# A backward pass on one TensorE: late loads and stores put on Sync's queue, parameter steps spread from another group on, and the opening of the last pass reordered

## The chip, the cores and the metric

The kernel runs on one core of one Trainium2 chip. The metric is the device time of one execution in microseconds. Engines are named as in the profile: PE (TensorE, with PEld for its weight loads), DVE (VectorE), ACT (ScalarE), POOL (GpSimd) and SP (Sync, which here only issues DMAs).

## The reference, cut to what matters

The reference is one block of a network and its gradients, with L = 2048 positions, D = 576 channels, N = 128 states, F = 4608 hidden units:

```
xn  = layernorm(x)
s   = ssm(xn)                      # convolution with K = sum_n C exp(dt A l) dt B, plus xn * Dskip
h   = silu(xn @ w1) * (xn @ w3)    # gate G, up U
out = x + s * silu(h @ w2)
outputs: out, and the gradients of x, A, B, C (re, im), log_dt, Dskip, w1, w3, w2
```

Three parts of the gradient matter here. With go the gradient at the output of h @ w2: gh = go @ w2.T; GG and GU, the gradients at xn @ w1 and xn @ w3, come from gh, G and U elementwise; grad w2 = h.T @ go, grad w1 = xn.T @ GG, grad w3 = xn.T @ GU. The gradient at xn is GG @ w1.T + GU @ w3.T (plus the convolution's part), followed by the layernorm's backward. And the gradients of A, B, C and log_dt need, for every channel, a sum over positions of the kernel's gradient times powers exp(dt A l).

## The kernel before, in words

A forward part (to some 700 us) writes G and U, the two hidden products, to DRAM by groups of 256 hidden units, position-major within the group. What follows is `backward` (L1521), in two stages.

**The group loop (L1599).** F is worked in NG = 18 groups of 256 units (numbered 0 to 17 here). For group gi:

- `phase6_group` (L1743) makes gh in four parts h0 to h3 (L1765, 40 matmuls each two parts), multiplies it into the prepared tiles gu and gg (L1783), and stores them as GU and GG (L1788, four DMAs on SP). After that comes the stage "stored".
- `phase6_grad2` (L1793), called at h1 and h3 for the group's two blocks of 128 units, makes grad w2 (L1806), copies it out of PSUM on ACT (L1810) and stores it to out_12 (L1811).
- `phase6_grad13` (L1813) makes grad w3 (out_11) and grad w1 (out_10), 64 matmuls each (L1826), with copies on ACT (L1828) and one store each (L1832), and a tail for the last 64 channels (L1836, L1838) whose two small stores (L1844, L1845) are issued at the beginning of the next group.
- Meanwhile the next group is prepared (`phase6_prep`, L1724): ACT computes silu(G) and its derivative (L1733, L1736), DVE the products with U (L1729, L1730).

For that, each group loads 1 MB of G (`phase6_load_gg`, L1704, for the next group, issued at the head of a group) and 1 MB of U (`phase6_load_h`, L1688, for the group after the next, issued after h3). In the kernel before, these two loads and all gradient stores are issued by POOL, chained in the order of the program (`gp`, L142). SP issues the rest: the rows of w2 (L1665), their transposes w2T (L1686, `nat_transpose`), the GU and GG stores, and from group GP = 11 on the loads for the parameter steps and the weight transposes wA ("end" of groups 11 to 15). From group 11 on `self.chain` holds SP's issues too in the order of the program (`sp`, L139); an engine's issue waits in that order for what it needs.

**Parameter steps.** `param_step` (L1230) does half a chunk of 8 channels: 8 matmuls (L1400), then on DVE two products (L1405) and two sums (L1408). There are 72 steps. A chunk's data are a DMA transpose qT, two loads gz and a load pz (`param_loads`, L1379), issued two chunks ahead. Steps stand at h1, h3, out_11, out_10 and "end" of the groups from 11 on, and in groups 12 to 15 at "stored" as well; in group 17 at h1, h3, out_11 and twice in the extra work at "stored". 39 steps are done in the groups, 33 in the last pass. The final blocks (`phase5_step`) turn finished sums into outputs.

**The last pass (`phase6_inputs`, L1852).** For each of 16 tiles of 128 positions it sums 72 pieces (36 of GG with w1.T, 36 of GU with w3.T; two matmuls of 288 columns each, L1876) in PSUM and then does the layernorm's backward. The activations of a tile (`acts`, one DMA transpose for GG and one for GU, `load_acts`, L1678) go into one of two buffers, so tile i+2's GG half can be loaded only when tile i has read its GG half. The weights come as transposed pieces (`load_piece`, L1668), which take over buffers of the group loop as these come free. The order of `steps` (L1857) is that in which the pieces were loaded, `sides` (L1858) is first all GG, then all GU. Tiles 0 and 1 take the order `steps`, all others `sides`. As L1888 to L1903 have it, tiles 0 and 1 are interleaved: each 49 pieces (what was loaded by the group loop), then each 9, then tile 0's last 14 and tile 1's last 14, with the loads for tiles 2 and 3 and the held parameter loads (`param_flush`, L1247) between. `stops` (L1910) says after which pieces a tile has parameter steps: three for tiles 3, 4, 6 and 8, four for tile 2, two for the others.

Of the kernel before, what the change touches and what calls it, by code (L numbers as in the profile page):

```python
# [17 lines left out]
P = 128  # L18
# [82 lines left out]
class K:  # L101
# [1128 lines left out]
    def param_step(self):  # L1230
# [3 lines left out]
        if self.half == 0:  # L1234
            for ch in range(2):
                self.loaded[ch] = self.param_loads(ch)
# [10 lines left out]
    def param_flush(self):  # L1247
        hold, self.hold = self.hold, None
        for ch in hold:
            self.loaded[ch] = self.param_loads(ch)  # L1250
# [270 lines left out]
    def backward(self, T0, TG, TQ, TC, TX, gctx, mats):  # L1521
# [11 lines left out]
        FA, GP = 14, 11  # L1533
        with ExitStack() as out:
# [22 lines left out]
            self.tail = None  # L1557
            self.at(T0 - TG)
# [40 lines left out]
            for gi in range(NG):  # L1599
                self.chain = gi >= GP  # L1600
# [103 lines left out]
    def phase6_load_gg(self, gi, inp):  # L1704
        gg = inp.tile([P, self.cfg.LT, self.FG], BF16, name="gg_n")
        self.gp(lambda: self.nc.gpsimd.dma_start(out=gg[:], in_=self.G_dram[gi]))
# [86 lines left out]
    def phase6_grad2(self, gi, fl, hn, gwp, ps_gw):  # L1793
# [6 lines left out]
        if True:  # L1800
# [10 lines left out]
            self.gp(lambda: nc.gpsimd.dma_start(out=aps["out_12"][fi * P:(fi + 1) * P, :], in_=gw2[:]))  # L1811

    def phase6_grad13(self, gi, gg_n, gu_n, gwp, ps_gw):  # L1813
# [7 lines left out]
        for (nat, oname) in ((gu_n, "out_11"), (gg_n, "out_10")):  # L1821
            gw = gwp.tile([P, nfull, FG], BF16, name="gw13", tag="gw13")
            for c in range(nfull):
# [6 lines left out]
                if (oname, c) in (("out_11", 2), ("out_10", 1)):  # L1830
                    yield oname
            self.gp(lambda: nc.gpsimd.dma_start(out=aps[oname][0:nfull * P, fb:fb + FG].rearrange("(c p) f -> p c f", p=P),  # L1832
                                                in_=gw[:]))
# [9 lines left out]
        def tail():  # L1843
            self.gp(lambda: nc.gpsimd.dma_start(out=aps["out_10"][nfull * P:D, fb:fb + FG], in_=gw[0:rem, :]))  # L1844
# [7 lines left out]
    def phase6_inputs(self, T2, TX, wT, acts, pool):  # L1852
# [7 lines left out]
        with pool(name="l_sb", bufs=2) as sb, pool(name="l_s1", bufs=1) as s1, \  # L1860
# [34 lines left out]
            for i in range(2):  # L1895
                product(i, opened[i][0], n1, n2, ())
# [160 lines left out]
```

## Time and profile before

| | |
|---|---|
| median of three timed runs | 1762.47 us (1759.99 to 1764.70) |
| the profiled execution | 1769.46 us |
| its span, first to last instruction | 1767.7 us |
| groups 11 to 17 of the group loop | 1161.2 to 1441.6 us of the span |
| the last pass, to its last matmul | 1441.6 to 1760.2 us |

Times in the profile are microseconds from the span's beginning. A row of a timeline has start, duration, engine, line, operation, output<-inputs and count, and in brackets how long the engine was idle before it and what ended the idle time. Rows of engine SP (SPq) are DMA issues; they last as long as SP is held by them. "To landing" is the time from a DMA's issue to its last byte. A matmul's modelled end overlaps the next one's start by about 0.16 us, so the time of a chain of them is read from the starts.

### The profile page before, as it was taken

The numbers are of one execution on the slowest core, as the hardware profiler recorded it, in microseconds if no ns is written. First come the engines' busy times: TensorE is split into PE (matmuls) and PEld (weight loads), VectorE is DVE, ScalarE is ACT, GpSimd is POOL, SyncE is SP. The second block draws the span as 40 slices with busy tenths as digits, with TensorE's granted clock in tenths as the row PEclk, the third lists the DMA queues.
The fourth block names the chain that finished last, engine by engine and source line by source line (L and its number), as shares of the span: only waits on it lengthen the run. The fifth ranks groups of instructions, "written<-read, shape, count | busy, mean of one in ns | idle before, by whom it ended". The sixth has DMA issues, their size and how long they took to land. (4 is left out here: it accounts for less than half of the span.)

```text
span 1767.7 us, 35373 instructions
## 1 busy us (share of the span) xinstructions
PE 1638.5 (93%) x13849; PEld 1206.2 (68%) x13909; DVE 1357.2 (77%) x2102; ACT 937.2 (53%) x1757; POOL 352.2 (20%) x579
## 2 busy tenths in 40 slices
PE   7789988999999999999989899999789997999998
PEld 2445544544535777788878788888678875778886
DVE  8768888795783554988966989569779975878675
ACT  5789999976863112776746676564444510000101
POOL 3112222223134110111111101111001143031132
PEclk9999999999999999999999999999889998999999
DMA  7889998889699988867664756689989999999992
GB/s 222 271 267 366 348 355 304 305 267 298 224 276 236 227 209 183 223 205 217 192 188 156 221 167 214 176 236 242 183 227 251 207 257 212 227 245 208 236 226 50
DMA packets 634718, 411.98 MB, mean 233 GB/s; under 512 B 424422, under 2 KB 579542, under 8 KB 629942
## 3 DMA queue, kind: packets, MB, share of 16 engines
q1 hardware_dynamic: 579676, 282.62, 63.4%
q0 software_dynamic: 32128, 107.99, 18.9%
q10 hardware_dynamic: 22746, 19.10, 3.9%
q8 instruction: 109, 1.79, 0.4%
q14 instruction: 59, 0.48, 0.1%
HBM read 130.88 MB, written 190.89 MB: 182 GB/s over the span
## 5 line engine op out<-in xcount | busy, mean ns | idle before, releaser
L1876 PEld LDWEIGHTS <-acts 128*128 128x128 bf16 x2304 | 225.9, 99 | 68.5 <-DMA acts<-GU_dram 6.8
L1826 PEld LDWEIGHTS <-xn_bf 128*128 128x128 bf16 x2304 | 224.5, 98 | 47.6 <-issue 21.1
L1405 DVE TENSOR_TENSOR pr_q<-et_ps,pz 128x1024 f32<-128x1024 f32 x144 | 175.8, 1221 | 43.0 <-PE et_ps L1400 36.1
L1876 PE MATMUL px<-wT,acts 128*128 128x288 bf16 x1472 | 189.3, 286 | 0.0
L1032 PEld LDWEIGHTS <-xnT 128*128 128x128 bf16 x1152 | 107.0, 98 | 112.2 <-issue 24.2
L1408 DVE TENSOR_REDUCE S_all<-pr_q 128x32 f32<-128x1024 f32 x144 | 175.1, 1216 | 3.1
L1765 PE MATMUL ph<-w2T,goT 128*128 128x256 bf16 x1440 | 174.6, 275 | 3.1 <-ACT gh L1768 3.1
L1032 PE MATMUL pg<-wmB_w,xnT 128*128 128x512 bf16 x545 | 149.1, 379 | 7.4 <-ACT g_t L1048 4.5
L1765 PEld LDWEIGHTS <-goT 128*128 128x128 bf16 x1440 | 140.6, 99 | 21.6 <-issue 4.5
L1806 PE MATMUL pgw<-go_o,h_n 128*128 128x288 bf16 x1152 | 151.8, 287 | 0.2 <-DVE h_n L1730 0.2
L1826 PE MATMUL pgw<-gu_n,xn_bf 128*128 128x256 bf16 x1152 | 136.8, 274 | 15.0 <-ACT gw L1810 13.3
L1032 PE MATMUL pu<-wmB_w,xnT 128*128 128x512 bf16 x553 | 149.9, 379 | 0.8
L1826 PE MATMUL pgw<-gg_n,xn_bf 128*128 128x256 bf16 x1152 | 130.8, 273 | 1.3 <-ACT gw L1828 1.3
L1806 PEld LDWEIGHTS <-h_n 128*128 128x128 bf16 x1152 | 112.4, 98 | 28.2 <-DVE h_n L1730 0.7
L1768 ACT CAST gh<-ph 128x512 bf16<-128x512 f32 x144 | 82.5, 603 | 89.9 <-PE ph L1765 79.9
L1876 PE MATMUL px<-wA,acts 128*128 128x288 bf16 x832 | 112.2, 293 | 10.2 <-DMA acts<-GU_dram 6.5
L1046 ACT ACTIVATE s_t<-pg 128x512 bf16<-128x512 f32 x144 | 88.0, 611 | 58.0 <-PE pu L1040 32.7
L679 ACT ACTIVATE cs_k<-et_ps 128x512 bf16<-128x512 int16 x216 | 111.6, 640 | 0.7 <-PE et_ps L677 0.7
L1932 ACT ACTIVATE go<-gx 128x576 bf16<-128x576 f32 x16 | 10.9, 683 | 189.7 <-DVE gx L1915 157.8
L1811 POOL DMA_DIRECT2D out_dram<-gw x36 | 19.8, 550 | 381.0 <-ACT gw L1810 200.3
L1729 DVE TENSOR_TENSOR gg_n<-gg_n,h_n 128x1024 bf16<-128x1024 bf16 x72 | 48.8, 683 | 57.0 <-ACT gg_n L1736 57.0
L1060 POOL DMA_DIRECT2D U_dram<-u_t x72 | 51.8, 720 | 203.6 <-ACT u_t L1051 196.7
(317 smaller groups left out, 3272.5 us busy)
## 6 DMA issues: line engine op xcount, KB each, us to landing
U_dram<-u_t POOLq DMA_DIRECT2D x72, 256.0 KB, 4.8
H_dram<-h_t SPq DMA_DIRECT2D x72, 256.0 KB, 4.9
G_dram<-g_t POOLq DMA_DIRECT2D x72, 256.0 KB, 5.0
Q_dram<-q_k SPq DMA_DIRECT2D x36, 512.0 KB, 4.7
gg_n<-G_dram POOLq DMA_DIRECT2D x18, 1024.0 KB, 5.8
h_n<-U_dram POOLq DMA_DIRECT2D x18, 1024.0 KB, 8.8
GG_dram<-gg_n SPq DMA_DIRECT2D x36, 512.0 KB, 10.1
GU_dram<-gu_n SPq DMA_DIRECT2D x36, 512.0 KB, 5.2
```

Of the source, the lines that this page charges most:

```text
L679: self.sin_last = nc.scalar.activation(out=CS[:, :, o:o + 256], in_=pt[:].bitcast(I16)[:, :, 0::2], func=ACT.Sin, scale=6.283184 / 2 ** 16)
L1032: ins = nc.tensor.matmul(pt[:], lhsT=xnT[:, c, ts], rhs=wm[w][:, c, :], start=(q == 0 and c == 0), stop=(q == 1 and c == nfull - 1))
L1046: nc.scalar.activation(out=s_t[:, :, q, :], in_=pgv, func=ACT.Silu)
L1060: self.u_stores[step] = nc.gpsimd.dma_start(out=dst[fb * ng:(fb + 1) * ng, :, i0:i0 + NT, :].rearrange("g p t f -> p g (t f)"), in_=src[:] ...
L1405: nc.vector.tensor_tensor(out=pr[:].rearrange("p r k e -> p r (k e)"), in0=T[x][:].rearrange("p z k h j a -> p (z k h j a)")[:, None].to_b ...
L1408: nc.vector.tensor_reduce(out=self.S_all[:].rearrange("p r (h c) -> p r h c", h=2)[:, :, :, d0:d0 + 2], in_=pr[:].rearrange("p r k (h j a) ...
L1729: nc.vector.tensor_tensor(out=gg[:, sl, :], in0=gg[:, sl, :], in1=hn[:, sl, :], op=ALU.mult)
L1765: self.pe_last = nc.tensor.matmul(ph[j][:, k, :].rearrange("p (a f) -> p a f", f=P), lhsT=lw, rhs=rh, start=(n == 0), stop=(n == nfull))
L1768: self.sc(lambda: nc.scalar.copy(out=gh[:, j], in_=ph[j][:]))
L1806: self.pe_last = nc.tensor.matmul(pgw[pi_][:, 0:pw], lhsT=hn[:, tt, fl * P:(fl + 1) * P], rhs=go_o[:, tt, po:po + pw], start=(tt == 0), st ...
L1826: self.pe_last = nc.tensor.matmul(pw_[:, 0:FG], lhsT=self.xn_bf[:, tt, c * P:(c + 1) * P], rhs=nat[:, tt, :], start=(tt == 0), stop=(tt == ...
L1876: self.pe_last = nc.tensor.matmul(px[pi_][:, 0:pw], lhsT=acts[i][:, ai, fi, :], rhs=w[:, po:po + pw], start=(n == 0), stop=(n == len(steps ...
```

## The change

It leaves every computation in place and moves instructions. Four parts:

1. From group 10 on the loads of G and U and the gradient stores are issued by SP. The G load is issued after h0 of a group, the stores at the next stage after they are recorded (`stores_due`). SP's chain begins in group 10, not 11.
2. Parameter steps begin in group 10 ("out_10" and "end"; the first two chunks are loaded at its "stored"), and the sixth step of groups 12 to 15 goes. 37 steps are done in the groups, 35 in the last pass, where tiles 3 to 8 have three each.
3. The pieces loaded late come in another order (GG's h_n piece, GG's gg_n piece, GU's w2T piece, GU's gu_n piece), the six last gradient stores stand between the first two, and tile 1's GU activations are loaded last.
4. Tile 0 takes 63 pieces in a row (all of its GG), then tile 1 its 36 GG pieces, tile 0 its 9 others, tile 1 its GU. Tile 1 takes the order `sides`. The loads for tiles 2 and 3 and the held parameter loads (one, then the rest) stand between.

```diff
@@ param_step, param_flush
-        if self.half == 0:
-            for ch in range(2):
-                self.loaded[ch] = self.param_loads(ch)
...
-    def param_flush(self):
-        hold, self.hold = self.hold, None
+    def param_flush(self, n=None):
+        hold = self.hold[:n]
+        self.hold = None if n is None else self.hold[n:]
         for ch in hold:
             self.loaded[ch] = self.param_loads(ch)
@@ backward
+            self.one_queue, self.gg_due, self.due = False, None, []
...
-                self.chain = gi >= GP
+                self.chain = self.one_queue = gi >= GP - 1
...
                 for stage in group if gi == 0 else self.phase6_group(gi, cur, elp, gwp, ps_h, ps_gw):
+                    self.stores_due()
+                    if stage == "h0" and self.gg_due:
+                        self.gg_due()
+                        self.gg_due = None
...
                     if stage == "stored":
-                        c = gi - GP
-                        if c in (1, 2, 3, 4):
-                            step()
+                        if gi == GP - 1:
+                            for ch in range(2):
+                                self.loaded[ch] = self.param_loads(ch)
...
-                            acts.append(self.load_acts(1))
+                            acts.append(self.load_acts(1, (0,)))
                             self.ready = sum(part[2] for part in wT)
-                            self.load_piece(wT, wp, "w2T", 1, 11, 2)
                             self.load_piece(wT, inp, "h_n", 0, 22, 7)
-                    elif stage in ("h1", "h3", "out_11", "out_10", "end") and gi >= GP and not (lastg and stage in ("out_10", "end")):
+                    elif stage in (("out_10", "end") if gi == GP - 1 else ("h1", "h3", "out_11") if lastg else
+                                   ("h1", "h3", "out_11", "out_10", "end") if gi >= GP else ()):
                         step()
...
             self.load_piece(wT, inp, "gg_n", 0, 29, 7)
+            self.load_piece(wT, wp, "w2T", 1, 11, 2)
             self.load_piece(wT, inp, "gu_n", 1, 29, 7)
+            self.load_acts(1, (1,), acts[1])
+            self.one_queue = False
+            self.stores_due()
@@ phase6_load_h, phase6_load_gg (alike, there with gg_due)
-        self.gp(lambda: self.nc.gpsimd.dma_start(out=hn[:], in_=self.U_dram[gi]))
+        if self.one_queue:
+            self.sp(lambda: self.nc.sync.dma_start(out=hn[:], in_=self.U_dram[gi]))
+        else:
+            self.gp(lambda: self.nc.gpsimd.dma_start(out=hn[:], in_=self.U_dram[gi]))
@@ the gradient stores of phase6_grad2 and phase6_grad13 now call
+    def grad_store(self, out, in_):
+        if self.one_queue:
+            self.due.append(lambda: self.sp(lambda: self.nc.sync.dma_start(out=out, in_=in_)))
+        else:
+            self.gp(lambda: self.nc.gpsimd.dma_start(out=out, in_=in_))
+
+    def stores_due(self):
+        for fn in self.due:
+            fn()
+        self.due = []
@@ phase6_inputs
-                    ai, fi, w = (steps if i < 2 else sides)[n]
+                    ai, fi, w = (sides if i else steps)[n]
...
-            n1, n2, n3 = self.ready, self.ready + 9, len(steps)
+            n1, n2, n3 = self.ready, self.ready + 14, len(steps)
...
             product(0, opened[0][0], 0, n1, (28,))
-            product(1, opened[1][0], 0, n1, ())
             for k in range(3):
                 self.phase5_step(self.half // 2)
-            for i in range(2):
-                product(i, opened[i][0], n1, n2, ())
-            for i in range(2):
-                product(i, opened[i][0], n2, n2 + 7, ())
-                acts.append(self.load_acts(i + 2, (0,), acts[i]))
-                product(i, opened[i][0], n2 + 7, n3, ())
-                if i == 0:
-                    self.param_flush()
-                self.load_acts(i + 2, (1,), acts[i])
+            product(0, opened[0][0], n1, n2, ())
+            acts.append(self.load_acts(2, (0,), acts[0]))
+            self.param_flush(1)
+            product(1, opened[1][0], 0, cfg.FT, ())
+            product(0, opened[0][0], n2, n3, ())
+            self.load_acts(2, (1,), acts[0])
+            acts.append(self.load_acts(3, (0,), acts[1]))
+            self.param_flush()
+            product(1, opened[1][0], cfg.FT, n3, ())
+            self.load_acts(3, (1,), acts[1])
...
-                stops = () if i in (0, 1, LT - 1) else (12, 28, 44, 62) if i == 2 else (14, 38, 62) if i in (3, 4, 6, 8) else (20, 50)
+                stops = () if i in (0, 1, LT - 1) else (12, 28, 44, 62) if i == 2 else (14, 38, 62) if 3 <= i <= 8 else (20, 50)
```

More of the change, by code (lines that the diff above doesn't have):

```diff
@@ L1705, in phase6_load_gg @@
         gg = inp.tile([P, self.cfg.LT, self.FG], BF16, name="gg_n")
-        self.gp(lambda: self.nc.gpsimd.dma_start(out=gg[:], in_=self.G_dram[gi]))
+        if self.one_queue:
+            self.gg_due = lambda: self.sp(lambda: self.nc.sync.dma_start(out=gg[:], in_=self.G_dram[gi]))
+        else:
+            self.gp(lambda: self.nc.gpsimd.dma_start(out=gg[:], in_=self.G_dram[gi]))
         return gg
@@ L1831, in phase6_grad13 @@
                     yield oname
-            self.gp(lambda: nc.gpsimd.dma_start(out=aps[oname][0:nfull * P, fb:fb + FG].rearrange("(c p) f -> p c f", p=P),
-                                                in_=gw[:]))
+            self.grad_store(aps[oname][0:nfull * P, fb:fb + FG].rearrange("(c p) f -> p c f", p=P), gw[:])
         pw_ = ps_gw.tile([P, 512], FP32, name="pgw")
@@ L1843, in tail @@
         def tail():
-            self.gp(lambda: nc.gpsimd.dma_start(out=aps["out_10"][nfull * P:D, fb:fb + FG], in_=gw[0:rem, :]))
-            self.gp(lambda: nc.gpsimd.dma_start(out=aps["out_11"][nfull * P:D, fb:fb + FG], in_=gw[rem:P, :]))
+            self.grad_store(aps["out_10"][nfull * P:D, fb:fb + FG], gw[0:rem, :])
+            self.grad_store(aps["out_11"][nfull * P:D, fb:fb + FG], gw[rem:P, :])
         self.tail = tail
```

4 lines of the change are left out of this document (3 added, 1 removed).

## The prediction

> **What bounds the kernel now.** I read the page's head first, then a table of the backward part by group.
>
> ```profile
> span 1767.7 us, 35373 instructions
> PE 1638.5 (93%) x13849; PEld 1206.2 (68%) x13909; DVE 1357.2 (77%) x2102; ACT 937.2 (53%) x1757; POOL 352.2 (20%) x579
> ```
>
> TensorE is busy for 1638.5 of 1767.7 us, so the change, which leaves every matmul in place, can only work on the other 129 us and on the clock. The view by windows, cut at the group borders, shows where they lie (columns: stretch, length, busy PE, PEld, DVE, ACT, POOL, granted clock, DMA share, GB/s). The rows are groups 11 to 17, then the last pass's first three tiles, then the rest of that pass.
>
> ```profile
> 1161.20:1196.00 34.80, 34.49 (x341) 29.95 (x340) 25.10 (x28) 19.72 (x32) 4.78 (x8) 1.00 0.77 216
> 1196.00:1233.20 37.20, 35.61 (x348) 30.41 (x344) 34.79 (x38) 19.46 (x32) 5.03 (x9) 1.00 1.00 245
> 1233.20:1287.40 54.20, 38.07 (x353) 31.95 (x354) 44.11 (x48) 19.40 (x31) 6.19 (x11) 0.86 1.12 196
> 1287.40:1327.30 39.90, 38.84 (x357) 32.62 (x358) 30.66 (x33) 19.20 (x31) 3.15 (x5) 0.93 0.87 214
> 1327.30:1365.30 38.00, 36.01 (x356) 30.85 (x354) 37.46 (x42) 19.40 (x32) 4.78 (x8) 1.00 0.99 246
> 1365.30:1400.80 35.50, 35.09 (x351) 30.59 (x349) 34.93 (x39) 19.70 (x32) 4.25 (x7) 1.00 0.87 203
> 1400.80:1441.60 40.80, 36.70 (x353) 30.91 (x350) 39.84 (x48) 11.30 (x25) 11.83 (x23) 1.00 1.12 256
> 1441.60:1510.60 69.00, 58.49 (x461) 45.11 (x460) 35.84 (x62) 5.31 (x11) 27.71 (x52) 0.90 1.04 228
> 1510.60:1760.20 249.60, 245.98 (x2128) 198.62 (x2125) 188.50 (x248) 25.34 (x49) 58.72 (x106) 1.00 0.99 202
> ```
>
> Group 16, with five parameter steps and nothing late, takes 35.5 us. Groups 12 and 15, with six, take 37.2 and 38.0; groups 13 and 14 take 54.2 and 39.9. The opening of the last pass takes 69.0. After that TensorE idles 3.6 us in 250. TensorE's timeline names the four long waits (in brackets: idle time, and what ended it):
>
> ```profile
> 1258.01 3.57 PE L1826 MATMUL pgw<-gu_n,xn_bf 128*128 128x256 bf16 x16 [8.01 <-ACT gw L1810]
> 1287.36 0.58 PE L1400 MATMUL et_ps<-gz,qT 128*128 128x128 bf16 x4 [7.30 <-DVE S_all L1408]
> 1482.20 6.04 PE L1876 MATMUL px<-wA,acts 128*128 128x288 bf16 x26 [3.69 <-DMA acts<-GG_dram]
> 1501.28 4.07 PE L1876 MATMUL px<-wA,acts 128*128 128x288 bf16 x18 [6.52 <-DMA acts<-GU_dram]
> ```
>
> The window around the first shows what such a wait costs further: TensorE comes back at a lower granted clock, 0.61 on average over these 13 us; the group rows above have it too (0.86, 0.93, 0.90).
>
> ```profile
> 1250.00:1263.00 13.00, 4.99 (x29) 3.48 (x28) 3.69 (x5) 1.39 (x3) 0.00 (x0) 0.61 1.08 155
> ```
>
> The first wait has its root in one load. ScalarE stood before the silu of the next group's G, and the PSUM copy L1810 stood behind that. The DMA list gives this G load 23.6 us to landing, another group's 7.0; on Sync's queue the wA transpose issued into it held the queue for 18.08 us, against 7.59 and 3.82 for both pieces in other groups.
>
> ```profile
> 1256.62 1.06 ACT L1733 ACTIVATE gu_n<-gg_n 128x1024 bf16<-128x1024 bf16 x1 [7.75 <-DMA gg_n<-G_dram]
> gg_n<-G_dram POOLq DMA_DIRECT2D x1, 1024.0 KB, 23.6
> gg_n<-G_dram POOLq DMA_DIRECT2D x1, 1024.0 KB, 7.0
> 1239.63 18.08 SPq L1686 DMA_TRANSPOSE wA<-in_B_w_dram  x1
> 1328.44 7.59 SPq L1686 DMA_TRANSPOSE wA<-in_B_w_dram  x2
> 1365.73 3.82 SPq L1686 DMA_TRANSPOSE wA<-in_B_w_dram  x2
> ```
>
> Everything behind it on Sync came some 15 us late, the parameter data of the step at 1287 among it: I read the second wait, though put down to VectorE, as the same event's second half.
>
> **The change part by part.**
>
> *Loads and stores on Sync's queue.* From group 10 on, per group, eight DMAs (1 MB of G, 1 MB of U, six stores with 0.9 MB of gradients) leave GpSimd's queue for Sync's, in order with the transposes. A load can no longer run into a transpose on another queue. If this removes the event, groups 13 and 14 fall to group 16's time: 54.2 - 35.5 = 18.7, and 39.9 - 35.5 = 4.4 us. Of these 23.1, the waits are 15.3, the sixth steps (below) some 2 each, which leaves 4 for the clock, 2 a wait.
>
> The new waits: in the new order Sync holds the store of out_10, wA, in every other group a parameter load (qT, gz, pz), the two tail stores, then the G load. These rows price them: out_10's store, the first and the last of a parameter load's four DMAs, a gradient store.
>
> ```profile
> 1363.95 0.76 POOL L1832 DMA_DIRECT2D out_dram<-gw  x1 [7.21 <-ACT gw L1828]
> 1361.36 2.39 SPq L1686 DMA_TRANSPOSE qT<-Q_dram  x1
> 1365.12 0.56 SPq L1389 DMA_DIRECT2D pz<-PZ_dram  x1
> L1811 POOL DMA_DIRECT2D out_dram<-gw x36 | 19.8, 550 | 381.0 <-ACT gw L1810 200.3
> ```
>
> Counted from the group's start (1365.3 in the first row), out_10's store ends at -0.6; wA takes 3.8, to 3.2; the parameter load 4.3 (1361.36 to 1365.68), to 7.5; tails 1.1, to 8.6; landing 7.0 later, at 15.6, or 11.3 without the parameter load. ScalarE wants it at 1256.62 - 7.75 = 1248.87, 15.7 after 1233.2. So 0.1 or 4.4 us are left; with wA at 7.6 the short case is 3.7 late, and behind ScalarE's silu stand the copies that free TensorE's accumulators, as at 1258. By the order of Sync's instructions groups 13 and 15 have the short case: between 0 and 2 x (3.7 + 2 of clock) = 11; I take 2, nearest to the row without a load beside wA. U's load waits for grad2's second half, but its data are wanted a group later: nothing. The GU and GG stores behind it come 2 to 4 us later; their readers are the last pass's loads, so only group 17 matters (below). GpSimd's own work between these DMAs is small (4.8 us in a group): no gain there.
>
> *Parameter steps from group 10.* Two steps move into group 10, groups 12 to 15 go from six to five, and two go to the last pass (33 to 35). A step is 8 matmuls (0.45 us) and, on VectorE, two products and two sums.
>
> ```profile
> L1405 DVE TENSOR_TENSOR pr_q<-et_ps,pz 128x1024 f32<-128x1024 f32 x11 | 13.4, 1219 | 2.2 <-PE et_ps L1400 1.8
> L1408 DVE TENSOR_REDUCE S_all<-pr_q 128x32 f32<-128x1024 f32 x11 | 13.4, 1214 | 0.2
> L1783 DVE TENSOR_TENSOR gu_n<-gh,gu_n 128x1024 bf16<-128x1024 bf16 x4 | 2.7, 680 | 0.0
> 1510.21 0.45 PE et_ps L1400 x8
> ```
>
> That is 2 x (1.219 + 1.214) = 4.87 us of VectorE. With a group's 16 products of 0.68 (10.9), six steps need 40.1, more than group 16's 35.5; five need 35.2. So groups 12 and 15 fall to 35.5: 1.7 + 2.5 = 4.2 saved. Group 11 rises by one step's 0.6 (34.8 to about 35.5), as the step of group 10's end now stands at its head; group 10 gains 0.5. All in all groups 11 to 16 go from 239.6 to 6 x 35.5 = 213: **-26.6**, and +0.5.
>
> In group 10 the first parameter loads, before issued ahead of the stores (qT at 1144.3), now stand behind the GG stores and one gradient store:
>
> ```profile
> 1144.30 2.41 SPq L1686 DMA_TRANSPOSE qT<-Q_dram  x1
> 1148.06 4.95 SPq L1788 DMA_DIRECT2D GG_dram<-gg_n  x2
> pz<-PZ_dram SPq DMA_DIRECT2D x6, 256.0 KB, 5.1
> ```
>
> qT then goes at 1153.6 and pz, 3.8 later, at 1157.4; it lands 5.1 on, at 1162.5. The instruction order has the step inside the tail matmuls, about 1160: 2.5, **+3** with some clock (0 to 5).
>
> *The last pass's opening.* Full-speed price: 432 matmuls at 7.35/60 = 0.1225, five steps and 0.7 of transposes: 52.9 + 2.3 + 0.7 = 55.9, against 69.0. The old waits go: tile 2's GG load can be issued once tile 0 has read 63 pieces, and tile 1's 36 GG pieces and 9 more of tile 0 (11.0 us) cover it. What is late next is a weight piece: tile 0 now goes straight on to piece 49 at 1441.6 + 12.0 + 1.2 = 1454.8, and to the gg_n piece at 1456.5. Sync's rows, and the landing of three pieces (median):
>
> ```profile
> 1445.27 6.70 SPq L1686 DMA_TRANSPOSE acts<-GU_dram  x1
> 1452.02 16.66 SPq L1686 DMA_TRANSPOSE wT<-in_B_w_dram  x4
> wT<-in_B_w_dram SPq DMA_TRANSPOSE x3, 8.3
> 1590.75 7.35 PE px L1876 x60
> ```
>
> Tile 1's GU (1445.27) gives its place to the 7-chunk h_n piece: 16.66 / 23 chunks x 7 = 5.1, to 1450.4; six stores at 0.55 (3.3) to 1453.7; the gg_n piece lands 8.3 later, 1462. Wait: 5.5, and 1.5 of clock. It is nothing if the stores and pieces run at DMA pace, 9 if Sync enters 2 later. I take 7 with the loads of step 40, so the opening is 63, **-6** (0 to -13).
>
> *Rest of the pass.* Two more steps, +0.9; tiles 5 and 7 now have three like their neighbours. VectorE has room there on average (188.5 of 249.6), but three steps take 14.6 of a tile's 144 x 0.1225 + 3 x 0.45 = 19.0, its own work and the final blocks come on top, and one wait of that kind stands in the trace:
>
> ```profile
> 1584.04 0.38 PE L1400 MATMUL et_ps<-gz,qT 128*128 128x128 bf16 x4 [2.57 <-DVE pr_q L1405]
> ```
>
> **+1.5** (-1.7, if that wait goes, to +6, if two more come).
>
> Sum: -26.6 + 0.5 + 2 + 3 - 6 + 1.5 = **-25.6**. The profiled execution took 1769.46 (span 1767.7 and 1.8 around it): 1743.9. The median of the timed runs is 1762.47, 7 below the profiled one; the event is worth 19 (23.1 less the sixth steps), so it cannot be missing from runs that are only 5 to 9 faster. 1762.5 - 25.6 gives 1737; I say **1738**.
>
> One sentence of the Trainium skill speaks against the largest term: "DMA: Bandwidth & Descriptors", section "Issuing engines are not separate DMA queues", says that DMAs from any engine run on the same 16 DMA engines and interleave, and that several issuing engines save only the time to issue. By that the choice of queue removes no collision, and the sum would be that of the first rival. The trace neither proves nor excludes it: the slow stretch occurred once, with both queues active, and five other G loads with both active were quick.
>
> **The rivals.**
>
> *The event comes from what the DMA engines carry, not from the queue.* For it: DMA share 1.12 in group 13, whatever the queue. Then 18.7 + 4.4 less the 4 of the sixth steps, 19, stay, and 1738 becomes 1757; if the opening gives nothing either, 1763.
>
> *Sync's queue becomes the bound; slower.* In group 15 Sync's 20 DMA issues from the wA at 1328.44 to the pz at 1365.12, fill 33.6 of 37.3 us.
>
> ```profile
> GB/s 222 271 267 366 348 355 304 305 267 298 224 276 236 227 209 183 223 205 217 192 188 156 221 167 214 176 236 242 183 227 251 207 257 212 227 245 208 236 226 50
> ```
>
> If these durations are Sync's own work, eight more DMAs (two loads of 2.9, an estimate from 1 MB at the best slice, 366 GB/s; four stores of 0.55, two of 0.76) add 9.5, half a parameter load less takes 2: 41 a group, 5.6 over TensorE's 35.5. Six groups: +34, so 1738 + 34 = 1772. It decides from where Sync's sum passes 35.5. Against it: the long rows are those with other traffic beside them (wA 7.59 and 3.82 for the same bytes), so most of the time is the DMA engines' and is counted already; their share at group 16 is 0.87.
>
> *The order doesn't change what ends last* (G's lateness was one-off, steps move without effect): about 1759.
>
> **How the numbers follow.** Forecast 0.66 (1722 to 1750); event stays 0.14 (1752 to 1763); Sync bound 0.15; no effect 0.05. A measurement of this kernel tells 0.3% (5.3 us) from no change. Faster by more (below 1757.2): 0.66 and half of the second case, 0.73; within: 0.10; slower: 0.17. The range reaches from the sum with the opening at 56, no wait in group 10, no late G load and group 17 without its 4.1 of idle TensorE (1738 - 7 - 3 - 2 - 4 = 1722) to the top of the second case, 1763; that leaves out the third case and a little of the first.
>
> **What would show it.** Right: groups 11 to 16 at 35 to 36 us each, no wait above 3 us on G; G landing within 9 us; VectorE below 36 in each. A short wait of TensorE at group 10's tail on qT, gz or pz. The opening at 56 to 66, with its wait now on a weight piece of tile 0 instead of acts. Wrong: a 15 us hold of a transpose on Sync anywhere in 1150 to 1440; ScalarE's silu waiting on G in several groups; Sync's rows without a gap and groups near 41 us.

## The result, and the profile after

The changed kernel takes 1776.86 us (median of 22 runs, 1768.65 to 1792.31); the kernel before, run beside it, 1772.72 (22 runs, 1753.58 to 1788.14). The ratio is 1.006, 95% interval 1.0031 to 1.0088: slower by 0.6%, where 1738 and a gain of 25.6 us were forecast. The ratios, here and below, are of fast runs alone: seven of the 22 runs of the kernel before lie more than 1.5% above its fastest and don't count in them, while the medians of all runs differ by 0.2%. Single runs of either kernel scatter by about 1%, so most of what follows reads stages of profiles, with the times beside them. The profiled execution took 1769.44 us with a span of 1767.7, the same span as in the profile of before. Its windows, cut at the group borders (rows: group 10, groups 11 to 17, the opening of the last pass, its rest; columns as before):

```profile
1125.80:1167.60 41.80, 37.33 (x344) 31.55 (x342) 24.54 (x43) 19.95 (x33) 0.00 (x0) 0.96 0.70 184
1167.60:1202.40 34.80, 34.49 (x342) 29.93 (x340) 31.75 (x34) 19.32 (x31) 0.00 (x0) 1.00 0.85 223
1202.40:1239.20 36.80, 35.15 (x349) 30.52 (x347) 33.19 (x37) 19.52 (x32) 0.00 (x0) 1.00 0.96 234
1239.20:1283.30 44.10, 36.81 (x347) 31.34 (x345) 33.12 (x37) 19.36 (x32) 0.00 (x0) 0.92 0.85 207
1283.30:1320.80 37.50, 35.05 (x348) 30.46 (x346) 33.11 (x37) 19.43 (x32) 0.00 (x0) 1.00 0.96 238
1320.80:1364.00 43.20, 37.63 (x348) 31.79 (x346) 32.98 (x37) 19.40 (x32) 0.00 (x0) 0.92 0.77 203
1364.00:1398.80 34.80, 34.80 (x349) 30.49 (x347) 34.18 (x38) 19.60 (x32) 0.00 (x0) 1.00 0.96 229
1398.80:1437.90 39.10, 36.59 (x352) 30.83 (x349) 38.09 (x47) 11.27 (x25) 9.36 (x18) 1.00 0.97 223
1437.90:1510.60 72.70, 57.99 (x450) 44.79 (x451) 35.54 (x62) 5.31 (x11) 25.43 (x49) 0.91 1.16 239
1510.60:1760.20 249.60, 247.49 (x2153) 200.11 (x2150) 198.10 (x256) 25.23 (x49) 58.46 (x106) 1.00 1.06 206
```

VectorE's 44.11 us of group 13 have come down to 33.12, and no group is at 54 any more. But groups 13 and 15 stand at 44.1 and 43.2, with five steps and a clock of 0.92, the opening is longer (72.7 us for 68.3), not shorter, and group 10 takes 41.8 (35.7 before, by the same borders). TensorE's timeline names the waits:

```profile
1163.63 0.69 PE L1398 MATMUL et_ps<-gz,qT 128*128 128x128 bf16 x8 [3.29 <-DMA gz<-gK_dram]
1220.40 1.25 PE L1850 MATMUL pgw<-gu_n,xn_bf 128*128 128x256 bf16 x10 [1.61 <-DVE gg_n L1796]
1262.76 1.23 PE L1850 MATMUL pgw<-gu_n,xn_bf 128*128 128x256 bf16 x5 [7.25 <-ACT gw L1823]
1302.05 1.14 PE L1850 MATMUL pgw<-gu_n,xn_bf 128*128 128x256 bf16 x9 [2.40 <-ACT gw L1823]
1342.73 1.23 PE L1850 MATMUL pgw<-gu_n,xn_bf 128*128 128x256 bf16 x5 [5.57 <-ACT gw L1823]
1464.25 1.36 PE L1899 MATMUL px<-wT,acts 128*128 128x288 bf16 x5 [7.42 <-DMA wT<-in_B_w_dram]
1502.93 1.01 PE L1398 MATMUL et_ps<-gz,qT 128*128 128x128 bf16 x8 [3.32 <-DMA gz<-gK_dram]
```

"ACT gw" is the copy that frees TensorE's accumulators; it stands behind ScalarE's silu, as at 1258 in the profile of before. What ScalarE waits for, and Sync's queue in the same group 13 (start 1239.2):

```profile
1260.07 1.28 ACT L1746 ACT_TABLE_LOAD   x1 [7.00 <-DMA gg_n<-G_dram]
```

```profile
1227.36 7.63 SPq L1801 DMA_DIRECT2D GG_dram<-gg_n  x2
...
1236.85 3.58 SPq L1693 DMA_TRANSPOSE qT<-Q_dram  x1
...
1243.42 4.44 SPq L1693 DMA_TRANSPOSE wA<-in_B_w_dram  x2
1247.96 2.89 SPq L1693 DMA_TRANSPOSE qT<-Q_dram  x1
...
1254.05 0.58 SPq L1717 DMA_DIRECT2D gg_n<-G_dram  x1
...
1267.32 0.33 SPq L1699 DMA_DIRECT2D h_n<-U_dram  x1
```

G lands 6.0 us after its issue (1254.05 to 1260.07), a good load. It is issued 14.9 us after the group's start: from 1227.36 to it Sync's rows follow one another without a gap (the rows left out are the rest of the parameter loads and the stores). ScalarE asked at 1260.07 - 7.00 = 1253.07, before the load was even issued. Then Sync itself stands 8.0 us before U's load for TensorE (the view of waits names the step's matmuls, L1398), which is late by now. The same in the opening: Sync comes to the first activations 32.4 us after group 17's start (1398.8), 27.6 before (1428.42), and the late stores stand between the weight pieces:

```profile
1431.16 4.85 SPq L1693 DMA_TRANSPOSE acts<-GG_dram  x1
...
1447.14 4.30 SPq L1693 DMA_TRANSPOSE wT<-in_B_w_dram  x1
1451.48 2.39 SPq L1828 DMA_DIRECT2D out_dram<-gw  x4
1453.96 1.54 SPq L1828 DMA_DIRECT2D out_dram<-gw13t  x2
1455.60 10.77 SPq L1693 DMA_TRANSPOSE wT<-in_B_w_dram  x3
```

### The profile page after: what moved, and what is told of

Same layout as the page of the kernel before. It is cut to its first block, busy times and chain, and to the rows that moved or that the text cites. A ratio compares the mean times of both kernels' runs of the same rounds, so it can differ in the third digit from the quotient of the medians.

```text
span 1767.7 us, 35351 instructions
## 1 busy us (share of the span) xinstructions
PE 1638.1 (93%) x13849; PEld 1207.7 (68%) x13909; DVE 1358.4 (77%) x2102; ACT 937.4 (53%) x1757; POOL 314.4 (18%) x516
## 5 line engine op out<-in xcount | busy, mean ns | idle before, releaser
L1899 PE MATMUL px<-wT,acts 128*128 128x288 bf16 x1472 | 192.9, 289 | 7.4 <-DMA wT<-in_B_w_dram 7.4
L1955 ACT ACTIVATE go<-gx 128x576 bf16<-128x576 f32 x16 | 10.9, 683 | 209.0 <-DVE gx L1938 180.5
L1830 POOL DMA_DIRECT2D out_dram<-gw x40 | 26.2, 655 | 349.9 <-ACT gw L1852 166.3
```

What stands on the lines that cost most here:

```text
L1899: self.pe_last = nc.tensor.matmul(px[pi_][:, 0:pw], lhsT=acts[i][:, ai, fi, :], rhs=w[:, po:po + pw], start=(n == 0), stop=(n == len(steps ...
```

## The experiments

The theory after the result: **place in Sync's one queue.** The long group goes, but G is issued behind what else Sync has in order, and the opening is late for the same reason. The rivals: the DMA engines' total work is the bound in any order; the moved steps, or the new opening, cost by themselves; there was less to gain than the profile of before showed. All lengths below are read from the starts of TensorE's rows in each kernel's profile (us); "11 to 16" is the sum of these groups, the opening runs from TensorE's end of group 17 to the last step of tile 2 (after 62 of its 72 pieces), the rest from there to the last matmul. Each ratio is to the kernel before on the same chip; each length is of one profile. Where the expectations of no_queue, short_queue and early_short speak of the new opening or of the rest behind it, their figures end the opening one step too early, after 44 pieces of tile 2, which makes it some 5 us shorter and the rest as much longer than in this table.

| kernel | ratio (95%) | group 10 | 11 to 16 | opening | rest |
|---|---|---|---|---|---|
| before, three profiles | 1 | 35.7 each | 239.5, 226.6, 222.6 | 68.3, 67.8, 71.1 | 250.3, 250.1, 263.7 |
| changed | 1.006 (1.0031 to 1.0088) | 41.8 | 231.1 | 72.7 | 249.6 |
| steps_alone | 0.998 (0.9948 to 1.0014) | 45.5 | 211.6 | 68.0 | 263.9 |
| queue_alone | 1.007 (1.0031 to 1.0109) | 35.7 | 237.7 | 66.5 | 254.1 |
| opening_alone | 0.999 (0.995 to 1.0033) | 35.7 | 234.2 | 67.9 | 248.0 |
| g_first | 1.001 (0.9967 to 1.0054) | 41.8 | 219.3 | 68.8 | 263.2 |
| stores_back | 0.996 (0.9923 to 0.9989) | 44.1 | 217.4 | 68.7 | 247.5 |
| old_opening | 1.010 (1.0043 to 1.0162) | 40.1 | 231.2 | 67.7 | 266.3 |
| no_queue | 0.992 (0.9888 to 0.9959) | 45.1 | 211.6 | 69.2 | 252.8 |
| five_steps | 0.994 (0.9902 to 0.9968) | 35.7 | 211.6 | 67.7 | 267.6 |
| short_queue | 0.993 (0.9902 to 0.9965) | 44.0 | 212.1 | 67.5 | 248.0 |
| early_params | 0.989 (0.9848 to 0.9931) | 36.6 | 211.6 | 68.9 | 257.2 |
| early_short | 0.990 (0.9859 to 0.9932) | 36.5 | 211.6 | 67.6 | 251.4 |
| wA_late | one run | 35.7 | 244.2 | 69.1 | 256.4 |

### The parts alone

**before_again**, no edit. 

> The kernel before, unchanged, with a second profile. The forecast took 23.1 us from groups 13 and 14 of the profile of before (54.2 and 39.9 us against 35.5 to 38 beside them): one transpose stood while a load on GpSimd's queue went out. If that event is part of the kernel, it is there again: one or two of groups 11 to 16 above 45 us, and the six of them near 240 us. If it was an accident of one execution (the rival: there was less to gain than the forecast took), the six come to 215 to 225 us, and the time to about 1750.

Measured: 1762.03; group 13 at 41.7, the six groups at 226.6. In between: the event is there, at less than half its size.

**steps_alone**: the changed kernel without part 1 (and, in the lines left out, with the opening of before).

```diff
-                self.chain = self.one_queue = gi >= GP - 1
+                self.chain = gi >= GP - 1
...
```

> The kernel before with the parameter steps alone moved (loads from group 10, five steps a group, stops in tiles 3 to 8); loads and stores stay on GpSimd's queue, the opening is that of before. Theory (Sync's one queue is what gave the gain back): group 10 grows by 3 to 5 us from the wait for its first parameter loads, groups 12 and 15 shrink by about 1.5 each with five steps for six, and the long group of before stays, somewhere in 11 to 16 (their sum 232 to 240): the time within 5 us of before. Rival (the moved steps are what makes the changed kernel slower): 5 us slower or more, with waits in groups 12 to 15 on G as in the changed kernel.

Measured: 1763.03, and both theories missed. With G on GpSimd's queue as before there is no long group at all, every one from 11 to 16 at 34.8 or 35.5. Group 10 pays 9.8 for the late first loads, and the rest of the pass 13.6, most of it in waits for gz (before_third, below, has such a rest too, 263.7, without a moved step). Rows: group 13, group 10's wait, the rest, its longest wait.

```profile
1241.30:1276.90 35.60, 35.29 (x349) 30.54 (x347) 33.21 (x37) 19.49 (x32) 4.75 (x8) 1.00 0.92 254
```

```profile
1162.35 0.80 PE L1398 MATMUL et_ps<-gz,qT 128*128 128x128 bf16 x6 [6.53 <-DMA gz<-gK_dram]
```

```profile
1489.70:1754.00 264.30, 249.78 (x2153) 200.37 (x2150) 198.91 (x258) 25.13 (x49) 58.96 (x107) 0.99 1.07 195
```

```profile
1623.78 0.61 PE L1398 MATMUL et_ps<-gz,qT 128*128 128x128 bf16 x8 [3.80 <-DMA gz<-gK_dram]
```

**queue_alone**: part 1 alone.

```diff
-                self.chain = gi >= GP
+                self.chain, self.one_queue = gi >= GP, gi >= GP - 1
...
```

> The kernel before with the late G and U loads and gradient stores alone moved to Sync's queue; steps and opening as before. Theory: no group above 46 us, but G is issued 9 to 15 us after the start of groups 12 to 15 and silu waits for it in two or more of them, with TensorE waits of 5 to 7 us; and since the late stores of the last group stand ahead of the pieces, the opening (start of the last pass to the last step of tile 2) grows from 68.4 to 72 or more: within 5 us of before, more likely above. Rival (the queue is not the fault, the new opening is): groups 11 to 16 come to 215 us or less and the time to 15 to 20 us below before.

Measured: 1780.86. As the theory had it for the groups: none above 43.1, but 42.5, 43.1 and 42.1 in groups 12 to 14, G issued 9.9 to 11.8 us after the start of 12 to 15. The waits are shorter than expected (two of 3.8 and 3.3 us are the longest), and the opening, 66.5, did not grow, against the theory. Sync comes to its activations 29.1 us after group 17's start (32.4 in the changed kernel), and the old order has its two long products ahead of what waits for the pieces behind the stores; which of these spares it isn't shown.

```profile
1298.72 0.53 SPq L1718 DMA_DIRECT2D gg_n<-G_dram  x1
```

```profile
1244.02 0.58 PE L1401 MATMUL et_ps<-gz,qT 128*128 128x128 bf16 x4 [3.81 <-DVE S_all L1409]
```

**opening_alone**: parts 3 and 4 alone (the changed kernel; the lines left out undo part 2).

```diff
-                self.chain = self.one_queue = gi >= GP - 1
+                self.chain = gi >= GP
...
```

> The kernel before with the new order of the last pass's pieces and of its first two tiles alone. Theory: with Sync not behind, the opening keeps what the forecast took from it: 68.4 becomes 62 to 66 us, the groups are those of before, and the time falls by 3 to 6 us. Rival (the new order is itself what costs): the opening comes to 72 us or more, as in the changed kernel, with the same chain of waits on the activations' and the weight pieces' transposes, and the time is 3 to 5 us above before.

Measured: 1765.5, and neither theory holds. The opening takes 67.9, hardly less than in the kernel before, and the interval of the time's ratio includes 1. The wait on a weight piece that was forecast is there (1.30 and 4.04 us). But a third one follows: the second step of tile 2, after 28 pieces, waits 4.07 us for VectorE. Rows: the opening, the wait on the piece, that of the step, then what VectorE and ScalarE had stood for.

```profile
1439.00:1506.90 67.90, 57.89 (x451) 44.78 (x452) 33.24 (x61) 5.31 (x11) 27.34 (x52) 0.92 1.17 249
```

```profile
1460.05 0.88 PE L1901 MATMUL px<-wT,acts 128*128 128x288 bf16 x3 [4.04 <-DMA wT<-in_B_w_dram]
1495.16 0.58 PE L1401 MATMUL et_ps<-gz,qT 128*128 128x128 bf16 x4 [4.07 <-DVE pr_q L1406]
```

```profile
1493.15 0.82 DVE L1973 SCALAR_TENSOR_TENSOR go<-gx,rstd,gxs 128x576 bf16<-128x576 f32 x1 [7.47 <-POOL gxs L1968]
1489.72 0.68 ACT L1957 ACTIVATE go<-gx 128x576 bf16<-128x576 f32 x1 [7.96 <-DMA odd_out<-go]
```

VectorE has the step's products behind the end of tile 0's and tile 1's layernorm backward. It waits there for GpSimd, GpSimd for ScalarE, and ScalarE for the store of tile 0's output. In the profile of before TensorE has done both steps by 1493 without such a wait, and then waits 6.52 us for activations.

So alone neither the steps (0.998) nor the opening (0.999) can be told from no change by the time; the queue move is the part that costs (1.007).

### The place in the queue

**g_first**: the changed kernel, G's load ahead of wA and of the last step's parameter loads.

```diff
+                if self.gg_due:
+                    self.gg_due()
+                    self.gg_due = None
+                if 0 <= gi - 1 - GP < cfg.DT:
+                    for part in wT[0:2]:
+                        self.load_wT_rows(part, gi - 1 - GP)
+                if gi > GP - 1:
+                    step()
...
```

> The changed kernel with one thing moved: on Sync's queue the load of G for the next group stands at the head of the group, ahead of wA's transposes and of the parameter loads of the step at the group's end (in the changed kernel it stands behind them); the other engines' order is the same. Theory (place in the one queue): G is issued within 5 us of the group's start in every group, the waits of TensorE on gw's copies in groups 13 and 15 (7.24 and 5.57 us in the changed kernel) and the 1.6 to 2.4 us in 12 and 14 go, and groups 11 to 16 come from 231.5 to 212 to 218 us; the time 5 to 15 us below the changed kernel, if the last pass doesn't take it back. Rival (the DMA engines' total work is the bound, in whatever order): G is issued early, lands late, or the stores and w2T behind it hold the group: the sum stays above 225.

Measured: 1769.24. Nothing but the order of Sync's queue is changed, and 231.1 becomes 219.3, a little above the 212 to 218 of the theory and below the 225 of the rival: groups 12, 13 and 15 fall to 35.5. But G is not within 5 us of the start in every group. Group 14 stays at 40.6, as Sync is late there before it comes to G at all (11.8 us after the start):

```profile
1284.86 0.46 SPq L1719 DMA_DIRECT2D gg_n<-G_dram  x1
```

```profile
1293.29 1.01 PE L1852 MATMUL pgw<-gu_n,xn_bf 128*128 128x256 bf16 x4 [3.86 <-ACT gw L1825]
```

**stores_back**: the changed kernel, gradient stores back on GpSimd.

```diff
     def grad_store(self, out, in_):
-        if self.one_queue:
-            self.due.append(lambda: self.sp(lambda: self.nc.sync.dma_start(out=out, in_=in_)))
-        else:
-            self.gp(lambda: self.nc.gpsimd.dma_start(out=out, in_=in_))
+        self.gp(lambda: self.nc.gpsimd.dma_start(out=out, in_=in_))
```

> The changed kernel with the gradient stores alone back on GpSimd's queue; G and U loads stay on Sync's. Theory: seven issues fewer a group on Sync shorten its backlog, but a part of it (parameter loads, w2T, wA, GG and GU stores) stays ahead of G: G is issued 5 to 10 us after the group's start instead of 11 to 15, the TensorE waits of groups 13 and 15 halve; groups 11 to 16 come to 217 to 226 us. Rival (it is the loads that are late whatever stands before them): no change, 229 to 234.

Measured: 1761.17, as the theory had it. G is issued 8.4 to 10.9 us after the start in groups 12 to 15, the waits of 7.25 and 5.57 shrink to 1.81 and 1.24 (the row is group 14's, 1.90), and the opening falls from 72.7 to 68.7: the stores on Sync cost it 4.0.

```profile
1296.66 0.71 PE L1847 MATMUL pgw<-gu_n,xn_bf 128*128 128x256 bf16 x5 [1.90 <-ACT gw L1823]
```

**short_queue**: both cures together. 

> The changed kernel with both cures of the queue: G's load at the group's head on Sync, and the gradient stores back on GpSimd. With each alone groups 11 to 16 came to 219.3 and 217.4 us. Theory: the waits are the age of G's load, and both together bring it to within 5 us of the group's start in all six: 211 to 214 us, opening 63 to 66 us, the time that of the same kernel without any queue move, 1752 to 1759. Then the queue move has nothing to win, only to lose. Rival (Sync's queue costs the last pass something even so): 1762 or more.

Measured: 1753.82, the groups at 212.1, the opening at 67.5, and in the rest TensorE has no wait above 0.8 us. As the theory had it: with a short enough queue the loads on Sync do no harm, and bring no time over GpSimd's queue. One thing stands against reading more into that: the rest is 4.8 us shorter than in no_queue, and the end of the kernel, behind the last matmul, 4.7 us longer (last section).

**no_queue**: the changed kernel without part 1 (new opening kept).

```diff
-                self.chain = self.one_queue = gi >= GP - 1
+                self.chain = gi >= GP - 1
```

> The changed kernel with loads and stores back on GpSimd's queue: the moved steps and the new opening together. From the two parts alone: groups 11 to 16 at 211 to 214 us as with the steps alone, group 10 at 43 to 46, the opening at 62 to 67 us with its waits on the second product's pieces. What is open is the end: with the steps alone TensorE waited 10 us more in the last pass (on gz, five times) than before. If that pass is bound by Sync's transposes, whose DMA share is above 1.05 in it, it takes a third to a half of the gain back: 1752 to 1760 us beside a before of 1768. If it isn't, 1743 to 1750.

Measured: 1756.25, the middle of what was expected for a pass that takes a part back. The opening is 69.2, longer than the 68.0 of the old order with the same steps; the rest is 252.8 for 263.9.

**old_opening**: the changed kernel with the opening of before. 

> The changed kernel with the opening of the last pass as it was before. Theory: the new opening is of no use when Sync comes late to it, so little changes: the opening 70 to 75 us (72.7 in the changed kernel), waits on the activations' transposes in place of those on the weight pieces, the time within 4 us of the changed kernel. Rival (the new opening costs 4 us of its own): the opening 68 to 69 us, the time 4 us lower.

Measured: 1784.37. In this profile the opening is shorter (67.7), as the rival had it, and the time is higher, which neither had: the rest takes 266.3, with one wait of 7 us on gz. That one profile doesn't say whether the new order helps the rest.

```profile
1642.37 0.80 PE L1398 MATMUL et_ps<-gz,qT 128*128 128x128 bf16 x6 [7.06 <-DMA gz<-gK_dram]
```

### What cures the long group, and what the first loads cost

**five_steps**: the kernel before, the sixth step moved to the last pass.

```diff
-                        c = gi - GP
-                        if c in (1, 2, 3, 4):
-                            step()
...
-                ... (14, 38, 62) if i in (3, 4, 6, 8) else (20, 50)
+                ... (14, 38, 62) if 3 <= i <= 10 else (20, 50)
```

> The kernel before with the sixth parameter step of groups 12 to 15 taken out and four stops added in tiles 5, 7, 9 and 10 of the last pass; nothing begins in group 10, queues and opening as before. The steps moved alone already took groups 11 to 16 from 239.5 to 211.6 us and left no long group, so the queue isn't needed for that. Theory: it is the sixth step's work on Sync and VectorE that makes Sync come late to wA and to the loads behind it; with five steps the groups are 34.8 to 35.7 us each and the six come to 211 to 214. Rival (it is the first loads that come a group earlier, or w2T two groups ahead from group 10, that cure it): a long group stays, the six above 222. The last pass has four steps more of some 1.5 us each, so the whole time is within 8 us of before on either.

Measured: 1756.33, the groups at 211.6 with every load on GpSimd. Taking out the sixth step is enough. G of group 13 lands after 5.6 us; VectorE's 33.2 leave room. But four more steps in the last pass make its rest the longest of all, 267.6. Group 13, and its G load:

```profile
1236.60:1272.20 35.60, 35.29 (x349) 30.52 (x346) 33.20 (x37) 19.47 (x32) 4.71 (x8) 1.00 0.92 246
```

```profile
gg_n<-G_dram POOLq DMA_DIRECT2D x1, 1024.0 KB, 5.6
```

**wA_late**: the kernel before, wA's transposes moved behind w2T of the same group. 

> The kernel before with wA's transposes alone moved on Sync's queue, from the head of groups 12 to 16 (while G's load is in flight) to behind w2T and w2's rows of the same group, some 15 to 20 us later. Theory (the event is the wA transpose beside G's load when Sync comes late to it): no transpose is held longer than 11 us in 1190 to 1330, G lands within 9 us, and groups 12 to 15 take 37 to 39 us each, groups 11 to 16 together 219 to 223. Rival (Sync is overfull with six steps, whichever transpose stands beside the load): another transpose, qT, is held 12 us or more, and the six take 226 us or more.

**before_third**, no edit. 

> The kernel before, unchanged, a third profile: the long group 13 again, between 41 and 55 us, with a wA transpose of 8 us or more in it; groups 11 to 16 together 226 to 240 us.

Measured: with wA away from it G's load of group 13 still takes 17.0 us and the groups 244.2 (1778.38 in all), now with waits on gz (10.5 and 6.2). So the first theory falls; the rival's sum of 226 or more is right, its long qT isn't there (7.92 at most). And before_third missed its expectation: group 13 at 38.0, G landing after 9.1. The G load of group 13 took 23.6, 12.5 and 9.1 us in three profiles of the kernel before, and 20.7 in opening_alone. First row wA_late, second before_third, then wA_late's wait:

```profile
gg_n<-G_dram POOLq DMA_DIRECT2D x1, 1024.0 KB, 17.0
```

```profile
gg_n<-G_dram POOLq DMA_DIRECT2D x1, 1024.0 KB, 9.1
```

```profile
1280.72 0.59 PE L1400 MATMUL et_ps<-gz,qT 128*128 128x128 bf16 x4 [10.54 <-DMA gz<-gK_dram]
```

**early_params**: no_queue, with the first two parameter loads at h1 of group 10.

```diff
+                    if stage == "h1" and gi == GP - 1:
+                        for ch in range(2):
+                            self.loaded[ch] = self.param_loads(ch)
...
```

> The moved steps and the new opening on the old queues (1756 us), with the first two parameter loads issued in the middle of group 10's h products instead of behind its stores, where Sync has been idle from 1117 to 1143 us. Theory (term c: the wait in group 10 is nothing but the age of the loads): the 6.0 us wait on gz goes, group 10 comes from 45.1 to 38 to 39.5 us, the rest of the groups stay at 211.6, and the time falls by 3 to 7 us, to about 1751. Rival (the last pass takes back what is won ahead of it, since Sync's queue has under 2 us of idle time in it): group 10 shortens, TensorE waits that much longer on gz in the last pass, and the time stays within 2 us.

Measured: 1744.69, the lowest of all here. The wait is gone and group 10 takes 36.6. In the profile, of an execution of 1752.28, half of that is given back in the rest (257.2 for 252.8), where acts now come late. Group 10, and the first qT (1151.16 in no_queue, with a group that starts 1.3 earlier):

```profile
1129.80:1166.40 36.60, 35.42 (x345) 30.60 (x343) 23.71 (x42) 19.88 (x33) 3.54 (x6) 1.00 0.75 207
```

```profile
1145.74 2.46 SPq L1693 DMA_TRANSPOSE qT<-Q_dram  x1
```

**early_short**: the same edit on short_queue. 

> The short queue (moved steps, new opening, G's load at the group's head on Sync, gradient stores on GpSimd) with the first two parameter loads issued in the middle of group 10's h products. Theory (the loads' age is all of group 10's wait; the queue of the loads no longer matters): group 10 comes from 44.0 to 37 to 39 us, groups 11 to 16 stay at 212, and the time is that of the same with loads on GpSimd's queue (1745, 0.989 of before) within 5 us. Rival (loads of G and U on Sync, in order with its transposes, help the last pass, where the short queue showed no wait of TensorE after the opening): the rest of the pass stays at 250 to 254 us against 262, and the time falls to 1738 or less.

Measured: 1745.8. By the time, as the theory had it, the queue of the loads no longer matters. The rival isn't excluded: the rest, 251.4, lies between those of short_queue and early_params (248.0 and 257.2), and the longer end of the kernel (last section) hides 4.7 us in the time.

## Why the prediction was wrong, point by point

From profile to profile, groups 11 to 16 came out 8.4 us shorter where 24.6 were forecast (late G included), the opening 4.4 longer where 6 shorter was forecast, and group 10 6.1 longer where 3.5 was. These three are the missing 25.6 us and 4 more, which group 17 (1.7 shorter) and the rest bring back.

- **The long group goes from Sync's queue: right, but not for the reason given.** The profile of before was its worst of three (239.5, 226.6, 222.6 for the six groups), so of the 26.6 us at most 11 to 15 were to be had in the other two. The argument that the event, at 19 us, couldn't be missing from runs 5 to 9 us faster fails: before_third has hardly any of it and took 1770.39, since its rest of the pass took 263.7. And the queue isn't needed: five_steps and steps_alone have 211.6 with G on GpSimd. The step to 35.5 us a group with five steps was right and is the whole cure; the 23.1 us were put down to the queue and belong to the sixth step. Moved alone, the queue leaves 237.7.
- **Late G: the step that failed.** It was priced at +2, 0 to 11. By the groups it is 231.1 - 211.6 = 19.5. The working let wA begin 0.6 us before the group's start, from rows of group 16, where Sync is ahead. In group 13 it begins 4.2 after it (1243.42), since the GG store held Sync 7.63 us and a parameter load stood ahead. With the forecast's own items from there, as they measured (wA 4.5, a parameter load 4.9, tails 1.2), G goes at 14.9 instead of 8.6, and lands at 20.9 against the 15.7 at which ScalarE wants it. g_first and stores_back show that this place in the queue costs 12 to 14 of the 19.5, short_queue that both cures together win all of it but 0.5.
- **Sync's queue as the bound, the rival that ends slower**, had the sign but not the shape: groups 11 and 16 stand at 34.8, none at 41 for want of Sync's time alone, and Sync waits 8.0 us for TensorE in group 13. It is latency in an in-order queue, not its length summed over a group.
- **Group 10's first loads: right in kind, half the size.** The wait on gz is there (3.29, forecast 2.5); group 10 grew by 6.1, not 3, and by 9.4 to 9.8 without the queue move. The GG stores ahead of the first qT held Sync 7.43 us, not the 4.95 of the working, so it went at 1157.3, not 1153.6. early_params shows that all but 0.9 of it is the loads' age.
- **The opening: the second step that failed.** -6 was forecast, and alone it is 67.9 for 68.3, 67.8 and 71.1. The weight pieces cost what was forecast (1.30 and 4.04 for 5.5). What the working put at nothing is VectorE at tile 2's second step: TensorE waits 4.07 to 7.70 us for it in all six kernels with the new opening in which Sync isn't late, and not at all in the profile of before. That chain is read from the trace; no run takes it out. The full-speed price was also 20 matmuls too long: it counts 432, to the end of tile 2, while the measured stretch ends after 412. In the changed kernel it is 72.7: Sync entered 4.8 us later than before, and TensorE waited 7.42 for the piece, within the 9 that the forecast allowed for a late Sync. The old order in the same company takes 67.7.
- **The rest:** +1.5 was forecast, -0.7 came in the profile. But the pass is no firm ground: 247.5 to 267.6 for the same pieces, by the waits on gz and acts. Opening and rest together are shorter with the new order in each pair (alone 315.9 for 317.9 to 334.8, with the steps 322.0 for 331.9, with the queue too 322.3 for 334.0), but the kernel before differs by 13.6 in the rest from profile to profile, so that isn't shown to be the order's doing. The DMA share of the rest is 0.99 to 1.09, Sync goes from transpose to transpose (in the changed kernel one gap of 0.43 us is the longest between its rows up to 1737), and what is won ahead of it comes back in part: steps_alone won 18 us to the start of group 17 and 6.6 in the span.
- **The Trainium skill's sentence** ("DMA: Bandwidth & Descriptors", section "Issuing engines are not separate DMA queues"), that the choice of issuing engine saves only issue time, is borne out where the loads are on time: 212.1 us with the loads on Sync, 211.6 on GpSimd. What decided here is the place in one engine's order: G stood behind 26.7 us of transposes, other loads and stores, and was issued 14.9 us into its group.

## What to carry to other kernels

Before a load is moved to a queue that issues in order, read at which time that queue comes to its place in the worst group, not in the best one, and put the load ahead of what can wait. Where a part removes a wait (the opening), read what the other engines do in the same stretch: the gain ends at the next one that is late. And time each part alone and with the rest, since lateness that one part brings falls on another. Last, an event seen in one profile is an event of one execution: a second profile of the same kernel tells what there is to gain.

## What was not expected of the hardware

- In the kernels with a sixth step and G on GpSimd's queue the G load of group 13 took 9.1 to 23.6 us to landing in five profiles of five (the 9.1 is of before_third, where two later G loads took 10.9 and 10.2); with five steps 5.6 to 6.4 in four of four. What happens in the DMA engines in that stretch stays open; wA_late has it without wA beside the load.
- A wait costs more than its length: group 13 of the changed kernel is 8.6 us over 35.5 for a wait of 7.25, group 15 7.7 for 5.57, both at a clock of 0.92. Groups 12 and 14 with waits of 1.61 and 2.40 kept 1.00. With 3.29 us, in group 10, it was 0.96. The Trainium skill ("TensorE: Matmul & The Clock Gate", section "HAM oscillation — how this bites in real kernels") puts the limit at idle gaps of more than about 3.4 us. The waits of the changed kernel come close to that, but the limit isn't sharp here: the granted clock was 0.50 for 3.42 us (1266.93 to 1270.35) behind a wait of 2.19 us in queue_alone, and 1.00 (1442.92 to 1449.00) behind one of 3.03 us in short_queue.
- The three kernels with the loads on Sync and the gradient stores on GpSimd (stores_back, short_queue, early_short) take 12.1 us from the last matmul to the end of the span, all others 7.4 to 7.7. In these three GpSimd's first closing instruction, a DRAIN, lasts 10.8 us, elsewhere 2.6 to 3.3, and the other engines wait for it. Why it lasts longer there isn't shown.
